# Threshold attention and a MetaFormer block on one core: layer-norm averages by token halves, and new places for the sums, squares and root around them

## The chip, the cores and the metric

One NeuronCore of a Trainium2 chip runs the whole program. The metric is the device time of one execution in microseconds; the table below gives the median of three. The core's engines run their own instruction streams in parallel: TensorE (PE in the profile; PEld is its loading of weights), VectorE (DVE), ScalarE (ACT), GpSimd (POOL) and SyncE (SP, which issues the transfers, DMAs). Work is handed from one engine to another by semaphores; SBUF is the on-chip memory, and PSUM the eight banks into which PE writes.

## The reference

Shapes: `q`, `k`, `v` are 8 batches x 8 heads x 576 tokens x 64; `x` is 8 x 576 x 512; `w_ch1` is 512 x 2048 and `w_ch2` 2048 x 512 (both weights arrive as 64-bit words and are converted in the kernel).

```python
scores = scale * np.matmul(q, k.transpose(0, 1, 3, 2))
thresh = np.max(scores, axis=-1, keepdims=True) - tau
scores = np.where(scores >= thresh, scores, -1000000000.0)
scores = scores - np.max(scores, axis=-1, keepdims=True)
attn = np.exp(scores)
attn = attn / (np.sum(attn, axis=-1, keepdims=True) + 1e-09)
attn_out = np.matmul(attn, v)
x = attn_out.transpose(0, 2, 1, 3).reshape(B, S, H * D)
mu = np.mean(x, axis=-1, keepdims=True)
var = np.mean((x - mu) ** 2, axis=-1, keepdims=True)
xn = (x - mu) / np.sqrt(var + 1e-06) * g_ln
ch = np.maximum(xn @ w_ch1, 0.0) @ w_ch2
return x + ch
```

## The kernel before

**Slots.** Attention runs in 72 slots, nine for each batch: four head pairs with the first 256 queries of each head, one slot with the last 64 queries of all heads, and four head pairs with the second 256. In a slot PE makes the scores (L434) into two PSUM tiles, `sc0` and `sc1`. DVE takes the row maximum, negated, of each (L450, `neg`). POOL makes thresholds from it (L454). ACT makes four exponentials (L463). DVE masks and sums them (L473, then two reciprocals), POOL divides (L490, four instructions), and DVE turns the result in 32 x 32 blocks (L559, two instructions). A DMA writes it to a scratch area in DRAM and another reads it back as `em`. In a later slot PE multiplies by the values (L638, L649), and at the begin of the slot after that ACT copies the two halves of the result to `x` (L663). One of these copies stands behind the first row maximum, at the place called "copy". POOL adds up the features (L692, `sums`), for the mean.

**Groups.** The MetaFormer block runs over 16 groups of `TOK` = 288 tokens, two for each batch, with features on the partitions (`NK` = 4 pieces of 128) and tokens along the rows. For a group `g`:

- `mean_of` (L701) multiplies the sums by `avg_sb`, a 128 x 128 matrix of 1/512, so that every partition gets the mean of each token. `product` (L98) does this in two matmuls, each for half of the output partitions, over all 288 tokens. The result stays in PSUM, and `centre` (L708) subtracts it from `x` with four DVE instructions.
- For groups 0 and 1, `first_part` (L988) makes the 16 pieces of `hidden` = relu(xc @ w_ch1) by plain products: `p1`, four products each, which ACT carries through a relu to `hidden` (L983, or L1008 for these two groups).
- From group 2 on, `first_units` (L955) makes eight pieces by plain `p1`s and eight by two units (`UNITS`), each in a slot of its own (`unit_slots`). A unit is a 2 x 2 product by Winograd's form of Strassen's scheme: seven products in place of eight, on sums and differences of the weights (`sums_of_w1` makes those once, during group 1) and of `xc` (`sum_x`, L859, makes `t1` to `t4`, two on DVE and two on POOL). Its results are brought together by DVE (L911) and ACT.
- The variance: ACT squares `xc` (L951), three POOL additions sum the four pieces (L953), PE averages them (L942), ACT adds epsilon and copies to SBUF (L944), and takes a logarithm and an exponential (L945, L946) for 1/sqrt. `root` (L776) refines that by one Newton step of three DVE instructions.
- `second_quarters` (L1046) makes hidden @ w_ch2 in seven `segment`s of 16 products of 144 tokens, again by Winograd's form. Sums of `hidden` (L1076) and of results (L1116) go to DVE and POOL, and `finish` (L1122) multiplies by `rb` and adds `x`; the results leave by `store`.

**The order.** The program fixes the order of instructions on each engine (`manual_schedule`, L149). The loop at L1326 goes through the slots, and `second_part` (L1222) deals steps of the group's generator `ffn_steps` into four quarters of each slot, after `STEPS` (the step count of each group), `ROOM` and `owed`. A generator yields a code and a cost after each step; unit steps stand in quarters 2 and 3 for the most part. `at_quarter(n, i, fn)` puts a call at a quarter of slot `n`; places -3, -2 and -1 stand around the scores, ahead of the row maximum. `later` (L1060) lines up DVE and POOL operations of the second part in `drops`; `drip` (L724) lets them go where there is room, and `need` (L1069) forces those that the next segment reads. `aside` holds calls that the loop lets go at fixed places (L1361, L1374, L1414, L1433), and `root` is one of them.

`ps_ff` has two PSUM buffers. Every `p1`, unit result, segment, mean and variance takes one of them in turn, so a product waits until the one before the last has been carried out. While `banks_taken` (L1134 to L1172) holds, means are put off to `waiting_mean`.

What `group_ready` (L1271) sets up for a group, in the slot ahead and in its first slot, is this:

```python
            at_quarter(*before, mean_of, g)
            at_quarter(*(first if g and first[1] else before), centre, g)
            if g > 1:
                at_quarter(first[0], 3 if first[1] else -1, sum_x, g)
        at_quarter(*first, lambda: queue.append(ffn_steps(g)))
```

From group 2 on, `ready` (L1215) is the begin of a slot, so `first` is that slot's quarter 0 and `before` the last quarter of the slot ahead; the two units stand in the slot `first[0]` and the one after it, called the first and the second unit slot below. So `mean_of` and `centre` run in the last quarter of the slot ahead, and `sum_x` at place -1 of the first unit slot, hence ahead of that slot's first row maximum on DVE. In group 1 the mean and `centre` are put among the steps of group 0 (`among`).

Of the kernel before, what the change touches and what calls it, by code (L numbers as in the profile page):

```python
# [18 lines left out]
def kernel(  # L19
# [679 lines left out]
    waiting_mean, banks_taken, among = [], [False], []  # L699

    def mean_of(g):  # L701
# [22 lines left out]
    def drip(room=None, everything=False):  # L724


        urgent = [i for i, d in enumerate(drops) if d[0]]
        n = urgent[-1] + 1 if urgent else 0
        room = dict(room or {})
        while drops:  # L730
            _, when, eng, cost, go = drops[0]
# [43 lines left out]

    def root(y, x, t):  # L776


        nc.vector.scalar_tensor_tensor(
            out=t, in0=y, scalar=-0.5, in1=y, op0=ALU.mult, op1=ALU.mult  # L780
        )
        nc.vector.tensor_mul(t, t, x)
        nc.vector.scalar_tensor_tensor(out=y, in0=t, scalar=1.5, in1=y, op0=ALU.add, op1=ALU.mult)
        rooted.append(y)

    rooted = []
    HT, HD, HM = TOK // 2, ND // 2, NK // 2
    early, late = slice(0, HT), slice(HT, TOK)
    w2 = {
# [68 lines left out]

    def sum_x(g):  # L859


        while g - 1 not in last_added:
            drops.pop(0)[-1]()
        xc = centred[g]
        part_of = lambda i, j: xc[:, 2 * i : 2 * i + 2, (early, late)[j]]
        (b11, b12), (b21, b22) = ([part_of(i, j) for j in range(2)] for i in range(2))
        t1, t2, t3, t4 = (
            ffn.tile([128, HM, HT], F32, tag="part", bufs=4, name=f"t{i}") for i in range(1, 5)
        )
        for eng, out, a, b in (  # L870
            (nc.vector, t1, b12, b11), (nc.gpsimd, t3, b22, b12),
            (nc.vector, t2, b22, t1), (nc.gpsimd, t4, b21, t2),
        ):
            eng.tensor_tensor(out=out, in0=a, in1=b, op=ALU.subtract)
        sums_of_x[g] = t1, t2, t3, t4

# [73 lines left out]
    def squares(sq, xc):  # L950
        nc.scalar.activation(sq, xc, func=AF.Square)  # L951
        for c in range(1, NK):
            nc.gpsimd.tensor_tensor(out=sq[:, 0], in0=sq[:, 0], in1=sq[:, c], op=ALU.add)  # L953

    def first_units(g):  # L955
# [32 lines left out]
    def first_part(g):  # L988


        xc = centred.pop(g)
        rb = sq = None
        plain = g == 0
        sums_of = differences() if g == 1 else iter(())
        for d in range(ND):
            while conversion.carried < 4 * (d // 4 + 1):
                yield 0, 0
            while d == ND - 2 and len(rooted) <= g and not plain:
                run_all(aside)
# [8 lines left out]
            nc.scalar.activation(hidden[:, d], p1, func=AF.Relu)  # L1008
            next(sums_of, None)
            yield 2, 1  # L1010
            if sq is None and d and (part > 1 or d == ND // 2 - 1):
                squared = d
                sq = hidden[:, ND - NK :]
                squares(sq, xc)
            elif sq is not None and rb is None and (
                d >= squared + (7 if plain else 3) and part > (0 if plain else 1)
                or d == ND - NK - 1
            ):
                two = [sq[:, c] for c in (2, 3)]
                if plain:  # L1020
                    two = [ffn.tile([128, HM, HT], F32, tag="part", bufs=4, name="two") for _ in two]
                    two = [t.rearrange("p m t -> p (m t)") for t in two]
                rb = variance(sq, two)
                yield 1, 1
        for _ in sums_of:
# [20 lines left out]
    def second_quarters(g, rb):  # L1046
# [13 lines left out]
        def later(*calls, urgent=None):  # L1060
            for what, cost, fn, eng, *args in calls:
# [4 lines left out]

                drops.append((urgent, now, eng, cost, go))

# [127 lines left out]
    ROOM = (0.6, 1.0, 1.25, 0.35)  # L1196
    STEPS = [1 + NK * ND * 2] + [1 + NK * ND * 2 - NK * ND // 8] + [
        1 + NK * ND * 2 - NK * ND // 8 - 2 * len(UNITS)
    ] * (NG - 2)
# [71 lines left out]
    def group_ready(g):  # L1271
# [203 lines left out]
```

## Time and profile before

| | us |
|---|---|
| median of three runs | 1356.83 |
| lowest and highest of them | 1356.06, 1356.85 |
| the profiled execution, its own time | 1358.76 |
| its span in the profile | 1357.0 |

| line, engine | what | count | busy, us | mean, ns |
|---|---|---|---|---|
| L434 PE | scores | 2048 | 139.7 | 403 |
| L638 PE | value products | 2368 | 130.9 | 265 |
| L103 PE | `seg` with `hidden` and w_ch2 | 3840 | 244.4 | 287 |
| L103 PE | `p1` and other first products of 288 | 2752 | 329.6 | 390 |
| L103 PE | `chain` of the units on `t` | 896 | 65.1 | 288 |
| L450 DVE | row maximum | 144 | 188.4 | 1349 |
| L473 DVE | mask and sum | 288 | 222.6 | 811 |
| L559 DVE | turning in blocks | 113 | 164.0 | 1452 |
| L463 ACT | exponentials | 288 | 195.6 | 752 |
| L490 POOL | division | 264 | 204.8 | 789 |
| L1128 POOL | `finish`, the product | 43 | 45.1 | 1048 |

How to read it: busy time is the sum over instructions of a line and a tile; the mean of one matmul holds its overlap with the next, since matmuls are pipelined. The profile also says for each instruction how long its engine stood idle ahead of it and which instruction of which engine released it. Times in a timeline count from the span's start. Two instructions on different engines that are shown at the same time did run side by side. The granted TensorE clock was 0.994 of full speed in the profiled execution.

### The profile page before, as it was taken

To read this page: it belongs to the slowest core of one execution; us is meant where nothing else is said; L and a number is where in the kernel's file an instruction comes from. 1 tells how busy PE (TensorE), PEld (TensorE's weight loads), DVE (VectorE), ACT (ScalarE), POOL (GpSimd) and SP (SyncE) were. 2 spreads that over 40 slices of the span, in tenths; PEclk is the share of its full clock that TensorE was granted. 3 is DMA by queue.
4 is the path that set the end of the run, shared out by engine and by line. 5 is a ranking of instruction groups with operands and counts; after the bars stand their busy time and mean duration, and the time that the engine had idled before them with its cause. 6 is when DMAs were issued, how large, how long until landed. Compare 5 with 4: busy or idle time off the path is not lost. (4 is left out here: it accounts for less than half of the span.)

```text
span 1357.0 us, 43410 instructions
## 1 busy us (share of the span) xinstructions
PE 1298.3 (96%) x18648; PEld 1052.8 (78%) x18648; DVE 959.7 (71%) x1700; ACT 479.3 (35%) x1051; POOL 651.6 (48%) x880
## 2 busy tenths in 40 slices
PE   8899899889999999999999999999999999999997
PEld 7765457769788797878879797887878788797977
DVE  7879885776867677776867768686777778677223
ACT  5866332142332414333332423324143333324120
POOL 3566555644545363454534455353634545444323
PEclk9999999999999999999999999999999999999999
DMA  8946864346744665545745467446664456453211
GB/s 159 299 114 170 214 175 151 140 135 191 193 150 146 185 166 167 188 150 128 204 150 185 138 190 192 150 146 186 166 179 170 149 134 187 150 185 115 80 19 19
DMA packets 335311, 214.11 MB, mean 158 GB/s; under 512 B 247376, under 2 KB 292688, under 8 KB 327056
## 3 DMA queue, kind: packets, MB, share of 16 engines
q1 hardware_dynamic: 329008, 210.46, 53.4%
q8 instruction: 146, 2.39, 0.7%
q10 hardware_dynamic: 5952, 0.74, 0.4%
q0 software_dynamic: 160, 0.15, 0.1%
q14 instruction: 45, 0.37, 0.1%
HBM read 124.00 MB, written 87.29 MB: 156 GB/s over the span
## 5 line engine op out<-in xcount | busy, mean ns | idle before, releaser
L103 PE MATMUL p<-xc,w 128*64 128x288 f32 (+1 forms) x2752 | 329.6, 390 | 17.0 <-ACT hidden L983 14.6
L103 PEld LDWEIGHTS p<-xc,w 128*64 128x64 f32 x2752 | 188.5, 137 | 143.6 <-ACT hidden L983 25.0
L450 DVE TENSOR_REDUCE neg<-sc 128x2 f32<-128x1152 f32 x144 | 188.4, 1349 | 108.7 <-PE sc L434 108.2
L490 POOL TENSOR_SCALAR e<-e,den 128x576 f32<-128x576 f32 x264 | 204.8, 789 | 119.3 <-DVE den L478 119.2
L103 PE MATMUL seg<-hidden,w 128*64 128x144 f32 x3840 | 244.4, 287 | 1.8 <-DVE hidden L1076 1.2
L103 PEld LDWEIGHTS seg<-hidden,w 128*64 128x64 f32 x3840 | 234.6, 137 | 11.6 <-issue 9.3
L473 DVE SCALAR_TENSOR_TENSOR e<-sc,thr,e 128x576 f32<-128x576 f32 x288 | 222.6, 811 | 22.4 <-POOL thr L454 10.5
L454 POOL TENSOR_SCALAR thr<-neg,low_sb 128x2 f32<-128x2 f32 x144 | 39.4, 274 | 347.7 <-DVE neg L450 347.5
L463 ACT ACTIVATE e<-sc,neg 128x576 f32<-128x576 f32 x288 | 195.6, 752 | 20.2 <-DMA scr<-e 13.3
L559 DVE STREAM_TRANSPOSE e<-e 128x1152 f32<-128x1152 f32 (+1 forms) x113 | 164.0, 1452 | 25.4 <-POOL e L490 24.6
L434 PE MATMUL sc<-kT,qT 64*64 64x384 f32 (+3 forms) x2048 | 139.7, 403 | 2.0 <-DVE e L473 1.6
L638 PE MATMUL sc<-em,v_in 128*64 128x128 f32 (+1 forms) x2368 | 130.9, 265 | 3.5 <-DMA em<-scr 2.9
L103 PE MATMUL seg<-hidden,stage 128*64 128x144 f32 x1920 | 126.0, 289 | 3.6 <-ACT part L1091 3.6
L638 PEld LDWEIGHTS sc<-em,v_in 128*64 128x64 f32 x2368 | 123.2, 138 | 6.3 <-issue 2.1
L103 PEld LDWEIGHTS seg<-hidden,stage 128*64 128x64 f32 x1920 | 119.0, 138 | 6.4 <-ACT part L1091 3.9
L1091 ACT COPY part<-seg 128x288 f32<-128x288 f32 x74 | 29.7, 405 | 229.0 <-PE seg L103 229.0
L434 PEld LDWEIGHTS sc<-kT,qT 64*64 64x64 f32 x2048 | 76.4, 133 | 43.0 <-issue 21.3
L663 ACT COPY x<-sc 128x128 f32<-128x128 f32 x120 | 31.6, 265 | 197.4 <-DVE neg L450 103.4
L1076 POOL TENSOR_TENSOR hidden<-hidden 128x576 f32<-128x576 f32 x60 | 84.0, 1419 | 24.6 <-ACT hidden L983 12.1
L1076 DVE TENSOR_TENSOR hidden<-hidden 128x576 f32<-128x576 f32 x60 | 52.5, 895 | 45.4 <-PE seg L103 39.0
L1128 POOL TENSOR_TENSOR y<-y,rb 128x288 f32<-128x288 f32 (+1 forms) x43 | 45.1, 1048 | 54.3 <-DVE y L1116 54.2
L103 PE MATMUL chain<-t,extra 128*64 128x144 f32 x896 | 65.1, 288 | 0.8
(163 smaller groups left out, 1615.9 us busy)
## 6 DMA issues: line engine op xcount, KB each, us to landing
scr<-e SPq DMA_DIRECT2D x60, 1152.0 KB, 5.0
em<-scr SPq DMA_DIRECT2D x63, 1024.0 KB, 5.7
out_dram<-ot SPq DMA_DIRECT2D x248, 36.0 KB, 3.9
q_in<-in_q_dram SPq DMA_DIRECT2D x120, 72.0 KB, 2.6
er<-scr SPq DMA_DIRECT2D x132, 64.0 KB, 5.2
k_in<-in_k_dram SPq DMA_DIRECT2D x116, 72.0 KB, 2.8
v_in<-in_v_dram SPq DMA_DIRECT2D x28, 256.0 KB, 5.5
w<-in_moe_w_ch_dram SPq DMA_DIRECT2D x10, 512.0 KB, 9.0
```

The lines of the kernel that those rows point to most:

```text
L103: nc.tensor.matmul(out[r], lhsT=lhsT[:, r], rhs=rhs, **flags)
L434: mm = nc.tensor.matmul(sc[h][64 * i : 64 * i + 64, at : at + n], lhsT=ql[r] if s == HP else qT[r, half, j * 128 + 64 * i : j * 128 + 64 * ...
L450: nc.vector.tensor_reduce(out=neg[:, i], in_=pairs[h], axis=AXL.X, op=ALU.max, negate=True,)
L454: nc.gpsimd.tensor_scalar(out=thr[:, i], in0=neg[:, i], scalar1=-1.0, scalar2=low_sb, op0=ALU.mult, op1=ALU.add,)
L463: nc.scalar.activation(blocks_of(es, i, n), like(blocks[i], n), func=AF.Exp, bias=neg[:, i : i + 1])
L473: nc.vector.scalar_tensor_tensor(out=e, in0=like(blocks[i], n), scalar=thr[:, i : i + 1], in1=e, op0=ALU.is_ge, op1=ALU.mult, accum_out=de ...
L490: nc.gpsimd.tensor_scalar(out=e, in0=e, scalar1=den[:, i : i + 1], scalar2=1.0, op0=ALU.mult, op1=ALU.mult,)
L559: nc.vector.transpose(et[:, :, at], et[:, :, at])
L638: mm = nc.tensor.matmul(dst[64 * h : 64 * h + 64], lhsT=vt[:, h, c, :], rhs=pick(em[:, 2 * j : 2 * j + 2, c], h), start=c == 0 and first, ...
L663: nc.scalar.copy(x_of(2 * b + (s > HP))[:, s % (HP + 1), 128 * j : 128 * j + 128], pv[j])
L1076: eng.tensor_tensor(out=out[at], in0=in0[at], in1=in1[at], op=op)
L1128: eng.tensor_tensor(out=z, in0=z, in1=r, op=ALU.mult)
```

## The change

It leaves what is computed as it is, and touches five things.

1. **Averages by token halves.** `average` replaces `product` for mean and variance. Each of its two matmuls takes 64 columns of `avg_sb` and 144 of the 288 tokens, so that the lower 64 partitions of the bank hold the early tokens' average and the upper 64 the late ones'. `spread` brings them to all 128 partitions of an SBUF tile, by four ACT instructions of 64 x 144; the variance's add epsilon at the same time, which took an instruction of its own. The mean is written over the sums that it came from (`spare` keeps the tile for the variance). In groups 0 and 1 the variance's average shares a bank with a `p1` (columns `TOK` and on), between its third and fourth product.
2. **`sum_x`** is called in two parts: `t1`, `t2`, `t3` on DVE, in the quarter of `centre` and behind it; `t4` on POOL in quarter 1 of the first slot. It waits there, by `drops`, for the last addition of the group before.
3. **Squares** go from the unit to the first unit slot's begin: ACT's square at place -3, two POOL sums at -1, the third in quarter 1. `root` works in place, in three DVE instructions as before, and is put at quarter 3 of the second unit slot (behind that slot's turning), in place of `aside`, which is emptied at the end of the first unit slot (L1433), ahead of the next row maximum on DVE.
4. **`sums_of_w1`** goes on by a piece in every 13th step of group 1's second part, not in every 8th.
5. **Around them:** `centre` lets go all of `drops` up to the additions "22" and "u4" of the group before; the last segment yields the bank for a waiting mean after 8 steps, not 12, and takes one more buffer in turn ("passed") behind the mean; the variance's step costs 0.5 and not 1, in `STEPS` too.

```diff
+    def average(to, bank, rhs, start, bias=None):
+        for h in range(2):
+            nc.tensor.matmul(
+                bank[64 * h : 64 * h + 64], lhsT=avg_sb[:, 64 * h : 64 * h + 64],
+                rhs=rhs[:, (early, late)[h]], start=start, stop=True, skip_group_check=True,
+            )
+        def spread():
+            for at in range(2):
+                for h in range(2):
+                    nc.scalar.activation(
+                        to[64 * at : 64 * at + 64, (early, late)[h]], bank[64 * h : 64 * h + 64],
+                        func=AF.Identity, **({"bias": bias[64 * h : 64 * h + 64]} if bias is not None else {}),
+                    )
+        return spread
+
     def mean_of(g):
...
-        means[g] = ps_ff.tile([128, TOK], F32, tag="ff", name="mean")
-        product(means[g], lhsT=avg_sb, rhs=sums.pop(g), start=True, stop=True)
+        bank = ps_ff.tile([128, HT], F32, tag="ff", name="mean")
+        means[g] = spare[g] = sums.pop(g)
+        average(means[g], bank, means[g], True)()
...
     def centre(g):
...
         mean = means.pop(g)
+        while any(d[4] in ("22", "u4") for d in drops):
+            drops.pop(0)[-1]()
...
-    def root(y, x, t):
+    def root(y, x):
+        nc.vector.tensor_mul(x, x, y)
         nc.vector.scalar_tensor_tensor(
-            out=t, in0=y, scalar=-0.5, in1=y, op0=ALU.mult, op1=ALU.mult
+            out=x, in0=x, scalar=-0.5, in1=y, op0=ALU.mult, op1=ALU.mult
         )
-        nc.vector.tensor_mul(t, t, x)
-        nc.vector.scalar_tensor_tensor(out=y, in0=t, scalar=1.5, in1=y, op0=ALU.add, op1=ALU.mult)
-        rooted.append(y)
+        nc.vector.scalar_tensor_tensor(out=y, in0=x, scalar=1.5, in1=y, op0=ALU.add, op1=ALU.mult)
...
-    def sum_x(g):
-        while g - 1 not in last_added:
-            drops.pop(0)[-1]()
+    def sum_x(g, which):
...
-        for eng, out, a, b in (
-            (nc.vector, t1, b12, b11), (nc.gpsimd, t3, b22, b12),
-            (nc.vector, t2, b22, t1), (nc.gpsimd, t4, b21, t2),
-        ):
-            eng.tensor_tensor(out=out, in0=a, in1=b, op=ALU.subtract)
-        sums_of_x[g] = t1, t2, t3, t4
+        t = sums_of_x.setdefault(g, [])
+        for i in which:
+            if i == 3:
+                while g - 1 not in last_added:
+                    drops.pop(0)[-1]()
+            t.append(ffn.tile([128, HM, HT], F32, tag="part", bufs=4, name=f"t{i + 1}"))
+            eng, a, b = (
+                (nc.vector, b12, b11), (nc.vector, b22, t[0]), (nc.vector, b22, b12),
+                (nc.gpsimd, b21, t[min(i, 1)]),
+            )[i]
+            eng.tensor_tensor(out=t[i], in0=a, in1=b, op=ALU.subtract)
...
-    def variance(sq, two):
-        var = ps_ff.tile([128, TOK], F32, tag="ff", name="var")
-        product(var, lhsT=avg_sb, rhs=sq[:, 0], start=True, stop=True)
+    def variance(g, sq):
+        x = spare.pop(g)
+        bank = ps_ff.tile([128, HT], F32, tag="ff", name="var")
+        average(x, bank, sq[:, 0], True, eps_sb)()
         rb = ffn.tile([128, TOK], F32, tag="rb", bufs=2, name="rb")
-        nc.scalar.activation(two[0], var, func=AF.Identity, bias=eps_sb)
-        nc.scalar.activation(rb, two[0], func=AF.Ln)
+        nc.scalar.activation(rb, x, func=AF.Ln)
         nc.scalar.activation(rb, rb, func=AF.Exp, scale=-0.5)
-        aside.append(lambda: root(rb, *two))
+        at_quarter(now // QUARTERS + 1, 3, root, rb, x)
         return rb
...
-                if g not in sums_of_x:
-                    sum_x(g)
-                if k == 0:
-                    squares(sq, xc)
                 yield from unit(g, xc, k)
                 k += 1
                 if k == 1:
-                    rb = variance(sq, [sq[:, c] for c in (2, 3)])
-                    yield 2, 1
+                    rb = variance(g, sq)
+                    yield 2, 0.5
...
-            p1 = ps_ff.tile([128, TOK], F32, tag="ff", name="p1")
+            bank = ps_ff.tile([128, 512], F32, tag="ff", name="p1")
+            p1 = bank[:, :TOK]
             for c in range(NK):
+                if due and c == NK - 1:
+                    x = spare.pop(g)
+                    spread = average(x, bank[:, TOK : TOK + HT], sq[:, 0], False, eps_sb)
+                    yield 1, 0.5
...
-        for _ in range(12):
+        for _ in range(8):
             yield next(last)
         banks_taken[0] = False
         while waiting_mean:
             mean_of(waiting_mean.pop(0))
+            ps_ff.tile([128, HT], F32, tag="ff", name="passed")
...
-            if i % 8 == 7:
+            if i % 13 == 12:
                 next(sums, None)
...
             if g > 1:
-                at_quarter(first[0], 3 if first[1] else -1, sum_x, g)
+                sq = hidden[:, ND - NK :]
+                at_quarter(*before, sum_x, g, (0, 1, 2))
+                at_quarter(
+                    first[0], -3,
+                    lambda: nc.scalar.activation(sq, centred[g], func=AF.Square),
+                )
+                at_quarter(first[0], -1, add_squares, sq, 1, 2)
+                at_quarter(first[0], 1, add_squares, sq, 3)
+                at_quarter(first[0], 1, sum_x, g, (3,))
```

More of the change, by code (lines that the diff above doesn't have):

```diff
@@ L699 @@
     waiting_mean, banks_taken, among = [], [False], []
+    HT = TOK // 2
+    early, late = slice(0, HT), slice(HT, TOK)
+    def average(to, bank, rhs, start, bias=None):
[12 more added lines that the diff above has]
+        return spread
     def mean_of(g):
@@ L704, in mean_of @@
             return
-        means[g] = ps_ff.tile([128, TOK], F32, tag="ff", name="mean")
-        product(means[g], lhsT=avg_sb, rhs=sums.pop(g), start=True, stop=True)
+        bank = ps_ff.tile([128, HT], F32, tag="ff", name="mean")
+        means[g] = spare[g] = sums.pop(g)
+        average(means[g], bank, means[g], True)()
+    spare = {}
     def centre(g):
@@ L730, in drip @@
         while drops:
-            _, when, eng, cost, go = drops[0]
+            _, when, eng, cost, _, go = drops[0]
             if n <= 0 and not everything:
@@ L774, in send @@
             )
-    def root(y, x, t):
+    def root(y, x):
+        nc.vector.tensor_mul(x, x, y)
         nc.vector.scalar_tensor_tensor(
-            out=t, in0=y, scalar=-0.5, in1=y, op0=ALU.mult, op1=ALU.mult
+            out=x, in0=x, scalar=-0.5, in1=y, op0=ALU.mult, op1=ALU.mult
         )
-        nc.vector.tensor_mul(t, t, x)
-        nc.vector.scalar_tensor_tensor(out=y, in0=t, scalar=1.5, in1=y, op0=ALU.add, op1=ALU.mult)
-        rooted.append(y)
-    rooted = []
-    HT, HD, HM = TOK // 2, ND // 2, NK // 2
-    early, late = slice(0, HT), slice(HT, TOK)
+        nc.vector.scalar_tensor_tensor(out=y, in0=x, scalar=1.5, in1=y, op0=ALU.add, op1=ALU.mult)
+    HD, HM = ND // 2, NK // 2
     w2 = {
@@ L866, in sum_x @@
         (b11, b12), (b21, b22) = ([part_of(i, j) for j in range(2)] for i in range(2))
-        t1, t2, t3, t4 = (
-            ffn.tile([128, HM, HT], F32, tag="part", bufs=4, name=f"t{i}") for i in range(1, 5)
-        )
-        for eng, out, a, b in (
-            (nc.vector, t1, b12, b11), (nc.gpsimd, t3, b22, b12),
-            (nc.vector, t2, b22, t1), (nc.gpsimd, t4, b21, t2),
-        ):
-            eng.tensor_tensor(out=out, in0=a, in1=b, op=ALU.subtract)
-        sums_of_x[g] = t1, t2, t3, t4
+        t = sums_of_x.setdefault(g, [])
[9 more added lines that the diff above has]
+            eng.tensor_tensor(out=t[i], in0=a, in1=b, op=ALU.subtract)
     def unit(g, xc, k):
@@ L938, in unit, with add_squares @@
         yield 2 if k else 3, 0.5
-    def variance(sq, two):
-        var = ps_ff.tile([128, TOK], F32, tag="ff", name="var")
-        product(var, lhsT=avg_sb, rhs=sq[:, 0], start=True, stop=True)
+    def variance(g, sq):
+        x = spare.pop(g)
+        bank = ps_ff.tile([128, HT], F32, tag="ff", name="var")
+        average(x, bank, sq[:, 0], True, eps_sb)()
         rb = ffn.tile([128, TOK], F32, tag="rb", bufs=2, name="rb")
-        nc.scalar.activation(two[0], var, func=AF.Identity, bias=eps_sb)
-        nc.scalar.activation(rb, two[0], func=AF.Ln)
+        nc.scalar.activation(rb, x, func=AF.Ln)
         nc.scalar.activation(rb, rb, func=AF.Exp, scale=-0.5)
-        aside.append(lambda: root(rb, *two))
+        at_quarter(now // QUARTERS + 1, 3, root, rb, x)
         return rb
-    def squares(sq, xc):
-        nc.scalar.activation(sq, xc, func=AF.Square)
-        for c in range(1, NK):
+    def add_squares(sq, *which):
+        for c in which:
             nc.gpsimd.tensor_tensor(out=sq[:, 0], in0=sq[:, 0], in1=sq[:, c], op=ALU.add)
@@ L992, in first_part @@
         rb = sq = None
+        due = False
         plain = g == 0
@@ L997, in first_part @@
                 yield 0, 0
-            while d == ND - 2 and len(rooted) <= g and not plain:
-                run_all(aside)
-            p1 = ps_ff.tile([128, TOK], F32, tag="ff", name="p1")
+            bank = ps_ff.tile([128, 512], F32, tag="ff", name="p1")
+            p1 = bank[:, :TOK]
             for c in range(NK):
+                if due and c == NK - 1:
+                    x = spare.pop(g)
+                    spread = average(x, bank[:, TOK : TOK + HT], sq[:, 0], False, eps_sb)
+                    yield 1, 0.5
                 product(
@@ L1008, in first_part @@
             nc.scalar.activation(hidden[:, d], p1, func=AF.Relu)
+            if due:
+                due = False
+                spread()
+                rb = ffn.tile([128, TOK], F32, tag="rb", bufs=2, name="rb")
+                nc.scalar.activation(rb, x, func=AF.Ln)
+                nc.scalar.activation(rb, rb, func=AF.Exp, scale=-0.5)
+                aside.append(lambda: root(rb, x))
             next(sums_of, None)
@@ L1013, in first_part @@
                 sq = hidden[:, ND - NK :]
-                squares(sq, xc)
+                nc.scalar.activation(sq, xc, func=AF.Square)
+                add_squares(sq, 1, 2, 3)
             elif sq is not None and rb is None and (
@@ L1018, in first_part @@
             ):
[L1019 to L1024, printed above, removed]
+                due = True
         for _ in sums_of:
@@ L1065, in go @@
                     done.add(what)
-                drops.append((urgent, now, eng, cost, go))
+                drops.append((urgent, now, eng, cost, what, go))
         def need(*what):
@@ L1196 @@
     ROOM = (0.6, 1.0, 1.25, 0.35)
-    STEPS = [1 + NK * ND * 2] + [1 + NK * ND * 2 - NK * ND // 8] + [
-        1 + NK * ND * 2 - NK * ND // 8 - 2 * len(UNITS)
+    STEPS = [0.5 + NK * ND * 2] + [0.5 + NK * ND * 2 - NK * ND // 8] + [
+        0.5 + NK * ND * 2 - NK * ND // 8 - 2 * len(UNITS)
     ] * (NG - 2)
```

## The prediction

> **What bounds the kernel now.** First the page's table of busy time: TensorE (PE) is the only engine near its limit.
>
> ```profile
> PE 1298.3 (96%) x18648; PEld 1052.8 (78%) x18648; DVE 959.7 (71%) x1700; ACT 479.3 (35%) x1051; POOL 651.6 (48%) x880
> ```
>
> So only two things are worth time: PE work taken away, and PE's idle time (58.7 us). Second, the view of waits for PE, its two largest rows (in all, times, longest):
>
> ```profile
> PE p L103 <- ACT hidden L983: 14.6, 26, 3.0
> PE chain L103 <- ACT hidden L983: 6.8, 12, 0.6
> ```
>
> PE wants a bank of `ps_ff` (two buffers) whose last product ScalarE (ACT) hasn't yet carried through L983. Third, the timeline of a group of odd number, on each engine, shows why ACT is late (start, busy, instruction, idle before and releaser):
>
> ```profile
> 663.76 2.12 PE L434 MATMUL sc<-kT,qT 64*64 64x384 f32 x32
> 665.81 4.10 PE L103 MATMUL p<-xc,w 128*64 128x288 f32 x32
> 670.50 1.20 PE L103 MATMUL chain<-xc,w 128*64 128x144 f32 x16 [0.59 <-ACT hidden L983]
> 672.07 1.20 PE L103 MATMUL p<-xc,w 128*64 128x144 f32 x16 [0.36 <-ACT hidden L983]
> 673.41 1.20 PE L103 MATMUL chain<-t,extra 128*64 128x144 f32 x16
> ...
> 680.96 2.12 PE L434 MATMUL sc<-kT,qT 64*64 64x384 f32 x32
> ```
>
> ```profile
> 664.68 1.66 DVE L874 TENSOR_TENSOR t<-xc 128x288 f32<-128x288 f32 x1
> 666.37 0.94 DVE L874 TENSOR_TENSOR t<-xc,t 128x288 f32<-128x288 f32 x1
> 667.23 2.61 DVE L450 TENSOR_REDUCE neg<-sc 128x2 f32<-128x1152 f32 x2
> ...
> 683.99 0.46 DVE L783 SCALAR_TENSOR_TENSOR rb<-hidden,rb 128x288 f32<-128x288 f32 x1
> 684.37 2.61 DVE L450 TENSOR_REDUCE neg<-sc 128x2 f32<-128x1152 f32 x2
> ...
> 701.35 2.62 DVE L450 TENSOR_REDUCE neg<-sc 128x2 f32<-128x1152 f32 x2 [5.53 <-PE sc L434]
> ```
>
> In the slot at 699.19 VectorE (DVE) is free: the row maximum begins 2.16 us after the scores begin, the first exponential 3.71 after, and PE never waits. In a group's first unit slot it begins 3.47 after (667.23), behind `sum_x` (L874); in the second 3.41 after (684.37), behind the root (L779 to L783). These 1.3 us pass on through the exponentials, which stand ahead of L983 on ACT.
>
> The price by start times, three `p1` at 701.24 to 707.11 giving 1.957 us each and 16 records of the unit 0.98. Odd groups: 0.78 + 0.59 + 0.36 + 0.05 = 1.78 us in the first unit slot (665.81 + 3.91 against 670.50, and so on), 0.72 + 0.58 + 0.06 = 1.36 in the second. Even groups: 0.90 (589.61 to 603.25) and 0.76 (609.86 to 617.47), since four and three `p1` stand ahead of their units. Below, an even slot is one of groups 2 to 14 (seven), an odd one of groups 3 to 13 (six); group 15 runs in the tail.
>
> **The averages.** PE spends 0.48 us on a mean (583.98 to 584.46), as much on a variance; two matmuls of 144 columns cost what one product of `seg` does, 16 records in 0.98, so 0.24. That two halves with different right sides run side by side is seen at L638: 32 records of 128 columns take 1.75, the same rate. Saved: 0.24 each. Four ACT spreads are new: no row shows 64x144, the rows below and above are 128x64 (0.215) and 128x288 (0.405); I take 0.27, near 128x128 (0.265), so 1.1 us a time, between 0.9 and 1.6.
>
> For the mean this lies in ACT's idle time: in the old trace ACT waits 5.83 us ahead of 663.69. The four subtractions of centring now start after the spread. In the slot ahead of an even group (16.5 us, scores at 571.09): mean done 12.85 after its scores, spread 13.95, four subtractions of 0.42, three sums of 0.45 (L874's 0.42 and 0.46 in the tail), done at 17.05. The next scores begin at 16.22 and the maximum at 18.4: 1.3 us to spare. Ahead of an odd group it is 1.8. That cover pays for the third sum (from POOL to DVE) too; without it each lost 0.1 us puts back 0.1 us of stall a group.
>
> A rule speaks against this: the Trainium skill, "GPSIMD Engine Reference", section "1. Specifications", says that POOL shares its SBUF interfaces with VectorE and contends with DVE instructions that have two SBUF inputs, which centring now becomes. The trace has that: 1.66 us at 664.68, beside a POOL add, against 0.42 at 1294.88 without one. By the rule with POOL busy throughout, centring would take 4 x 1.66 = 6.6 us, past all cover, and the sum below would lose its stalls; but POOL idles there (nothing from 658.7 to 662.9), and the two large POOL operations that followed (L1128, L1116 on 128x576) now stand behind the squares.
>
> **Even groups.** The first two sums of squares stand ahead of the thresholds on POOL: the square starts after the copy of `p3` (0.33 after the scores), ends at 1.5, two adds of 0.81 end at 3.2, the first threshold comes at 3.5: hidden. The maximum begins on time, so 0.90 and 0.76 vanish. The variance's longer tail on ACT ends 2.6 after the next scores, ahead of the exponential at 3.71. Root moved behind the turning falls into DVE's idle stretch (5.53 ahead of 701.35 in its like); nothing needs `rb` before the second half.
>
> **Odd groups, where I expect a new wait.** The changed order puts on POOL, between the second threshold and the divisions L490: scaling q 0.74, the last square 0.85, the two on 128x576 1.6 and 1.5, the fourth sum 0.85. These rows stand in the old trace at other places:
>
> ```profile
> 662.88 1.56 POOL L1128 TENSOR_TENSOR y<-y,rb 128x576 f32<-128x576 f32 x1 [4.19 <-DVE y L1116]
> 664.51 1.50 POOL L1116 TENSOR_TENSOR y<-y,x 128x576 f32<-128x576 f32 x1
> ...
> 673.62 1.46 POOL L490 TENSOR_SCALAR e<-e,den 128x576 f32<-128x576 f32 x2 [2.69 <-DVE den L478]
> ...
> 678.63 1.38 DVE L911 TENSOR_TENSOR hidden<-sc,hidden 128x288 f32<-128x288 f32 x3
> ```
>
> Counted from the scores: the second threshold starts at 4.88 (2.72 after the maximum, as at 669.95) and ends at 5.13; POOL is free at 10.7, DVE's two reciprocals at 9.0 and 10.7 (L1116 for `p3` moved ahead of them, 0.6). The four divisions run 10.7 to 13.6, the two transposes (1.38) end at 15.0, and the unit's sums L911 (1.93 for all four) end at 16.9; old: 16.25. PE without its stalls would be through the unit at 14.6. It now waits for the first L911 (15.5, the bank of the variance), then, as the changed order pulls one `p1` forward, for ACT L934, which needs L911: 16.95. Next scores: 16.95 + 1.96 + 0.27 = 19.2, less the pulled `p1` 17.2: the old 17.20. Gain nothing, where 1.78 + 0.24 were to be had. Bounds: 2.0 if POOL is not in the way, minus 0.6 if each POOL step takes the longest row seen of its kind (1.0 for the 0.85s, 1.6 for both large ones).
>
> In the second odd slot one `p1` is left ahead of the unit. Its `p2` waits for L983 until 3.71 + 1.73 = 5.44 (as 668.77 to 670.50), wanted at 4.99: 0.45; the chain waits for L905 until 7.0, wanted at 6.42: 0.59. With 1.04 in place of 1.36 the gain is 0.32, between 0 and 1.36.
>
> **The rest.** Wider w_ch1's sums move DVE and POOL work of equal size; stalls of 3.6, 1.2, 2.4 and 3.0 us lie there (238 to 276). They are DVE's chain; what shortens it for certain is its end: adds, centring and sums took 7.46 us (265.37 to 272.83) beside POOL and would take 5.0. I take 2.4, between 0 and 10.3. In groups 0 and 1 the averages inside a `p1` save two 0.24s and perhaps 1.3 of stalls, but PE then waits longer for the weights (4.08 at 153): 0, between -1 and +2. In the tail PE's 0.57 wait for `part` ahead of 1291.90 goes, as the next product takes the mean's bank: 0.6.
>
> **Sum.** Even first slots 6 x 0.90 = 5.4 (group 2's is in the 2.4); even second 7 x 0.76 = 5.3; variances of even groups 7 x 0.24 = 1.7; means of groups 3 to 15, 13 x 0.24 = 3.1; odd second 6 x 0.32 = 1.9; odd first 0; group 1's end 2.4; tail 0.6. Together 20.4 us. The profiled execution took 1358.76 (span 1357.0 and 1.8 around it), 1.9 above the median of 1356.83; the gain is taken from the median: **1336.4**.
>
> **Rivals.** (a) POOL isn't in the way in odd groups, as it runs these steps beside DVE's: 6 x 2.0 = 12 more, 1324. For it: the divisions waited 2.69 for DVE before; against: the four steps sum to 4.8. (b) The maximum stays late, because four ACT instructions and centring from SBUF use up the 1.3 us: half of the stalls (6.3) stay, 1343. For it: ACT's spread has no row of its own; against: ACT and POOL idle there. (c) The wait merely changes its place, in even groups too: all but the PE work returns, 1352 to 1357. (d) Slower: POOL's steps ahead of the divisions are stretched by DVE. At 85.28 four divisions took 4.59 beside DVE where 2.91 is usual, 1.6 times; 4.8 us would become 7.7, 2.9 later. Odd slots lose 6 x 2.9, even ones, whose transposes have 1.45 of cover ahead of L911, 7 x 1.45: 27.5 against 20.4, so 1364; it decides from 2.4 us of stretch on. Against it: beside L473 at 578.6 the divisions kept 2.90.
>
> **How the numbers follow.** My forecast 0.58 (own range 1330 to 1341), (a) 0.16, (b) 0.13, (c) 0.04, (d) 0.09. The range runs from (a) to just past (b), 1323 to 1346, with (c) and (d) left out. About 0.2% (2.7 us) is what a measurement of this kernel tells from no change: faster 0.88, within 0.03, slower 0.09.
>
> **What would show it.** Right: L450 begins 2.2 us after L434 in every unit slot; PE's waits for L983 shrink from 21.4 us to about 6; mean and variance take 0.24; in odd first slots PE waits for L911 and L934 and the divisions start 10.7 after the scores. Wrong: L490 before 10 there (then (a)), L450 later than 2.5 ((b)), L911 past 18 ((d)).

## The result, and the profile after

The changed kernel takes 1337.57 us (median of four runs, 1336.1 to 1338.82) against 1356.84 before: 0.9857 of it, 95% interval 0.984 to 0.9874, so 19.3 us less. The forecast was 1336.4. Its profiled execution took 1336.10 (span 1334.0), the fastest of the four, and the one before 1358.76 (span 1357.0), slower than all four of its kernel, so the traces show 23.0 us of difference where the medians show 19.3.

The page's table of busy time: PE keeps the same number of instructions and loses 13.1 us of busy time, and POOL 10.7; ACT has 112 instructions more.

```profile
PE 1285.2 (96%) x18648; PEld 1052.7 (79%) x18648; DVE 947.3 (71%) x1714; ACT 515.0 (39%) x1163; POOL 640.9 (48%) x866
```

The view of waits for PE (in all, times, longest). The relu of `p1` is now L1002, the relu at a unit's end L958, the first chain copy L929:

```profile
...
PE p L103 <- ACT hidden L958: 4.8, 7, 0.7
PE sc L103 <- DVE e L473: 4.3, 6, 0.9
...
PE p L103 <- ACT hidden L1002: 2.9, 7, 1.4
...
PE chain L103 <- ACT hidden L929: 2.1, 6, 0.3
```

The 14.6 and 6.8 us of waits for the relu of `p1` are down to 2.9. Two new waits stand in their place, six and seven times: a unit's product waits for VectorE's masks (L473), and the `p1` that was pulled forward waits for the unit's last relu. Six of each belong to the odd groups' first unit slots (the seventh of the second stands in the tail), as PE's timeline of the same group as before shows (start, busy, instruction, idle before and releaser):

```profile
652.08 2.12 PE L434 MATMUL sc<-kT,qT 64*64 64x384 f32 x32
...
660.11 1.15 PE L103 MATMUL chain<-t,extra 128*64 128x144 f32 x16
661.94 1.20 PE L103 MATMUL sc<-t,w 128*64 128x144 f32 x16 [0.68 <-DVE e L473]
...
667.66 0.41 PE L708 MATMUL var<-hidden,avg_sb 128*64 128x144 f32 x4
668.78 2.16 PE L103 MATMUL p<-xc,w 128*64 128x288 f32 x16 [0.71 <-ACT hidden L958]
...
671.14 2.12 PE L434 MATMUL sc<-kT,qT 64*64 64x384 f32 x32
```

By start times the first wait is 661.94 - 660.11 - 0.98 = 0.85 and the second 668.78 - 667.66 - 0.24 = 0.88. DVE and POOL in the same slot tell where the masks were held up:

```profile
654.23 2.62 DVE L450 TENSOR_REDUCE neg<-sc 128x2 f32<-128x1152 f32 x2 [1.71 <-PE sc L434]
...
658.81 1.60 DVE L1142 TENSOR_TENSOR y<-y,part 128x288 f32<-128x288 f32 x1
660.33 0.81 DVE L473 SCALAR_TENSOR_TENSOR e<-sc,thr,e 128x576 f32<-128x576 f32 x1
```

```profile
657.21 0.74 POOL L350 TENSOR_SCALAR q_in<-q_in,scl_sb 128x576 f32<-128x576 f32 x1
657.92 0.80 POOL L976 TENSOR_TENSOR hidden<-hidden 128x288 f32<-128x288 f32 x1
658.67 1.42 POOL L1154 TENSOR_TENSOR y<-y,rb 128x576 f32<-128x576 f32 x1
660.17 1.51 POOL L1142 TENSOR_TENSOR y<-y,x 128x576 f32<-128x576 f32 x1
661.64 0.79 POOL L899 TENSOR_TENSOR t<-xc,t 128x288 f32<-128x288 f32 x1
662.42 2.90 POOL L490 TENSOR_SCALAR e<-e,den 128x576 f32<-128x576 f32 x4
```

The row maximum begins at 2.15 after the scores. The addition of the last segment (L1142 on DVE, 658.81) takes 1.60 us, four times its usual 0.42, and ends just after POOL's product (658.67 to 660.09). The divisions begin at 662.42, 10.34 after the scores.

Where the time came from, slot by slot (start of the scores to start of the next; slots counted from 0, as in the experiments below). The four rows from the even first unit slot to the other five slots stand for six such stretches each; with them the table makes up 22.6 of the 23.0 us:

| place | before | after | difference | foreseen |
|---|---|---|---|---|
| slots 0 to 13 | 226.62 to the end of slot 13 | 227.09 | +0.5 | 0 |
| slots 14 to 16 (group 1's end, group 2's first unit) | 64.85 | 59.27 | -5.6 | -2.4, and -0.2 for the variance |
| even first unit slot (34) | 20.25 | 19.08 | -1.17 | -0.90 - 0.24 |
| even second (35) | 19.59 | 18.84 | -0.75 | -0.76 |
| odd first and second (38, 39) | 35.43 | 35.05 | -0.38 | -0.32 |
| the other five slots of nine (two means) | 82.88 | 82.41 | -0.47 | -0.48 |
| from slot 71 to the end | 115.80 | 114.89 | -0.9 | -1.6 |

The first row gives the time at which slot 14 begins. It is the least steady part: among this study's profiles of kernels that are nearly alike up to there, it lay between 225.94 and 228.95, while most of the later slots repeat to some hundredths (a few single ones take up to some 1.2 us longer in one trace or another).

### The profile page after: what moved, and what is told of

Same layout as the page of the kernel before. It is cut to its first block, busy times and chain, and to the rows that moved or that the text cites. A ratio compares the mean times of both kernels' runs of the same rounds, so it can differ in the third digit from the quotient of the medians.

```text
span 1334.0 us, 43429 instructions
## 1 busy us (share of the span) xinstructions
PE 1285.2 (96%) x18648; PEld 1052.7 (79%) x18648; DVE 947.3 (71%) x1714; ACT 515.0 (39%) x1163; POOL 640.9 (48%) x866
## 4 chain that ended last, share of the span: by engine, by line
PE 72%; DVE 8%; POOL 7%; SPq 4%; ACT 4%; issue 3%; DMA 2%; POOLq 0%; DVEq 0%; ACTq 0%
PE seg L103 29%; PE p L103 15%; PE sc L434 9%; PE sc L638 7%; PE chain L103 6%; PE sc L103 3%; POOL e L490 2%; DVE neg L450 2%; ACT e L463 2%; PE sc L649 2%; SPq L120 1%; DVE e L473 1%; DVE extra L569 1%; DVE hidden L935 1%; DVE e L559 1%
## 5 line engine op out<-in xcount | busy, mean ns | idle before, releaser
L473 DVE SCALAR_TENSOR_TENSOR e<-sc,thr,e 128x576 f32<-128x576 f32 x288 | 222.5, 810 | 12.7 <-POOL thr L454 5.2
L454 POOL TENSOR_SCALAR thr<-neg,low_sb 128x2 f32<-128x2 f32 x144 | 46.3, 322 | 359.2 <-DVE neg L450 358.8
L976 POOL TENSOR_TENSOR hidden<-hidden 128x288 f32<-128x288 f32 x48 | 38.7, 807 | 77.9 <-ACT hidden L1311 76.4
L1002 ACT ACTIVATE hidden<-p 128x288 f32<-128x288 f32 x112 | 47.2, 422 | 50.9 <-PE p L103 50.7
```

The lines of the kernel that those rows point to most:

```text
L454: nc.gpsimd.tensor_scalar(out=thr[:, i], in0=neg[:, i], scalar1=-1.0, scalar2=low_sb, op0=ALU.mult, op1=ALU.add,)
L473: nc.vector.scalar_tensor_tensor(out=e, in0=like(blocks[i], n), scalar=thr[:, i : i + 1], in1=e, op0=ALU.is_ge, op1=ALU.mult, accum_out=de ...
```

## The experiments

Every kernel is the changed one with one edit (the third and the ninth are combinations) and was timed against the kernel before. The changed kernel's ratio is 0.9857.

**1. POOL's two large steps behind the divisions.** In the first unit slot, the search for the group before's last addition leaves POOL's product and addition on 128x576 ("hi") in the list.

```diff
                 while g - 1 not in last_added:
-                    drops.pop(0)[-1]()
+                    drops.pop(drops[0][4] == "hi")[-1]()
```

> The two large POOL steps of the group before (the product with rb and the addition of x, both 128x576) go behind the divisions in each first unit slot; nothing else moves. Theory: in the odd groups' first unit slots POOL's order sets the end. The addition on DVE no longer runs beside POOL's product, so the masks begin 7.2 us after the scores in place of 8.25, the divisions at 8.9 in place of 10.34, and the unit's sums end 1.5 earlier. Of PE's two waits there, that for the scores' tile (0.85 by start times) goes and that for the unit's last relu (0.88) falls to about 0.2; the slot takes 17.6 in place of 19.06, and 6 such slots give 9 us: 1328.5. Even groups' first slots (19.08, no wait) stay. Rival: the wait is set by ACT's chain and the order on PE, whatever POOL does first: slot 18.9 or more, time 1336 to 1339.

Measured: 1330.4, ratio 0.9801 (0.9787 to 0.9814). Slot 38 takes 17.86. DVE's timeline there, with the scores at 649.00:

```profile
655.73 0.41 DVE L1142 TENSOR_TENSOR y<-y,part 128x288 f32<-128x288 f32 x1
656.07 0.81 DVE L473 SCALAR_TENSOR_TENSOR e<-sc,thr,e 128x576 f32<-128x576 f32 x1
```

With no product on POOL at that moment the same addition takes 0.41; the masks begin at 7.07 and the divisions at 8.93, as expected. The wait for the masks is gone from PE; that for the last relu is 0.58 by start times, where 0.2 was expected, so the slot stays 0.26 above the 17.6 that was worked out and the time 2 us above. Even first slots stay at 19.08, though their divisions too come 2.6 earlier: there they have cover. So POOL's order set the end of the odd first slot in the changed kernel, and the rival falls.

**2. The pulled `p1` put back.** The variance's step counts 1 for groups 2 to 15.

```diff
-                    yield 2, 0.5
+                    yield 2, 1
...
-        0.5 + NK * ND * 2 - NK * ND // 8 - 2 * len(UNITS)
+        1 + NK * ND * 2 - NK * ND // 8 - 2 * len(UNITS)
```

> The variance's step counts 1 again and not 0.5 for groups 2 to 15, so in the odd groups one p1 goes back from the first unit slot to the second; averages, sums, squares and root stay as changed. Theory: the p1 pulled forward pays twice, by waiting for the unit's last relu in the first slot (0.88) and by leaving a single p1 ahead of the second unit (0.99 of waits there). With it back the first slot takes 16.4 to 16.7 (its scores wait some 0.4 for the unit's sums that read their tile) and the second 16.95 without a wait: 33.5 for the two in place of 35.05, 6 times, 1328.5. Rival: the wait only moves to the next scores and comes back whole: 34.9 to 35.1 for the two, 1336 to 1339.

Measured: 1327.85, ratio 0.9782 (0.9769 to 0.9795). Slots 38 and 39 take 16.59 and 17.04, 33.6 for the two. Half a step in a table of costs had moved one `p1` by a slot, at a price of 1.4 us in each odd group.

**3. Both edits together.**

> Both edits, POOL's two large steps behind the divisions and the p1 back in the second slot. Theory: the waits of both odd unit slots go, 15.4 and 16.95, 32.35 in place of 35.05; 6 x 2.7 = 16 us: 1321. Rival (the two gains are one and the same wait): as the better of the two alone, 1328 to 1330; or, if neither matters, 1336 to 1339.

Measured: 1321.29, ratio 0.973 (0.9716 to 0.9743). The odd pair takes 15.38 and 17.04 (slots 20 and 21) with no wait. The gains add up, 7.2 and 9.7 alone, 16.3 together. In one group slot 39 takes 18.03: ACT's first exponential waits 0.94 there for the `scr` transfer that still reads the attention weights' tile, so there a transfer is next. This is the fastest version of the study, with experiment 9, from which it can't be told apart.

**4. Squares back in the unit.** The square and three POOL sums run behind the exponentials and divisions again.

```diff
+                if k == 0:
+                    nc.scalar.activation(sq, xc, func=AF.Square)
+                    add_squares(sq, 1, 2, 3)
                 yield from unit(g, xc, k)
...
-                at_quarter(
-                    first[0], -3,
-                    lambda: nc.scalar.activation(sq, centred[g], func=AF.Square),
-                )
-                at_quarter(first[0], -1, add_squares, sq, 1, 2)
-                at_quarter(first[0], 1, add_squares, sq, 3)
```

> The squares and their three POOL sums go back to where they stood, into the unit's slot behind the exponentials and the divisions. Theory (the squares' move is worth little by itself, since POOL's time ahead of the divisions is what counts): in odd first slots the divisions begin 0.8 earlier, 9.5, and the wait for the last relu shrinks by 0.8, while ACT's square of 1.2 ahead of the chain's copy adds 0.4 to 0.5 of wait there: about -2 us in all, even slots plus or minus 0.2: 1333 to 1339. Rival (the move is what made the even slots free of waits): ACT's square delays the chain's copy in all 13 first slots by 1.2 or the variance comes late: 1345 to 1353.

Measured: 1332.47, ratio 0.9816 (0.9802 to 0.9829), a little better than the theory's range. The divisions of slot 38 begin at 9.60 and the slot takes 18.33; even first slots take 19.19, 0.11 more. So this part of the change, by itself, makes the changed kernel slower: it puts POOL work ahead of divisions that set the end.

**5. The root back ahead of the row maximum.**

```diff
-        at_quarter(now // QUARTERS + 1, 3, root, rb, x)
+        aside.append(lambda: root(rb, x))
```

> The root goes back to the end of the first unit slot, ahead of the next row maximum on DVE; all else as changed. Theory: DVE's order decides. In even groups rb now comes 3.29 us after the second unit slot's scores (the variance has four spreads on ACT where it had one copy), so the root ends at 4.7 and the maximum, which began at 2.16, begins at 4.7; that is 1.3 later than in the kernel before, where the wait was 0.76, so some 2.0 a group, 7 times 2.0 = 14. In odd groups rb comes 0.87 after the scores and the root is done by 2.3: nothing. Time 1347 to 1353. Rival: three p1 stand ahead of the unit and hide it, as does ACT's own lateness: 1336 to 1341.

Measured: 1352.77, ratio 0.9965 (0.9953 to 0.9976). DVE and PE in slot 35, scores at 603.34:

```profile
606.66 0.46 DVE L806 TENSOR_TENSOR sum<-sum,rb 128x288 f32<-128x288 f32 x1 [3.54 <-ACT rb L970]
...
608.03 2.62 DVE L450 TENSOR_REDUCE neg<-sc 128x2 f32<-128x1152 f32 x2
```

```profile
611.30 2.16 PE L103 MATMUL p<-xc,w 128*64 128x288 f32 x16 [1.81 <-ACT hidden L1002]
```

DVE idles 3.54 us for `rb`, the maximum begins 4.69 after the scores, and PE loses 2.0: the slot takes 20.87 for 18.84. Odd second slots lose 0.1. 15 us hang on this one place. That is more than the root cost in the kernel before (0.76 a group), since `rb` now comes later, behind the four spreads.

**6. Averages over 288 tokens again.** The mean is read from PSUM, the variance brought over by one ACT instruction.

```diff
-        bank = ps_ff.tile([128, HT], F32, tag="ff", name="mean")
-        means[g] = spare[g] = sums.pop(g)
-        average(means[g], bank, means[g], True)()
+        means[g] = ps_ff.tile([128, TOK], F32, tag="ff", name="mean")
+        spare[g] = sums.pop(g)
+        product(means[g], lhsT=avg_sb, rhs=spare[g], start=True, stop=True)
...
-        bank = ps_ff.tile([128, HT], F32, tag="ff", name="var")
-        average(x, bank, sq[:, 0], True, eps_sb)()
+        var = ps_ff.tile([128, TOK], F32, tag="ff", name="var")
+        product(var, lhsT=avg_sb, rhs=sq[:, 0], start=True, stop=True)
+        nc.scalar.activation(x, var, func=AF.Identity, bias=eps_sb)
```

> From group 2 on (and all means) an average is one product of 288 tokens again, the mean read by centring from PSUM, the variance brought over by one ACT instruction; groups 0 and 1 keep the variance inside a p1. All else as changed. Theory: PE's work alone counts, 0.24 each: 14 means and 7 variances of even groups cost 5.0 more, variances of odd groups nothing, as PE waits behind them for the unit's last relu anyway: 1341 to 1344. Rival: the four spreads on ACT, and centring from SBUF beside POOL, eat up what PE saves: 1335 to 1338.5.

Measured: 1340.95, ratio 0.9876 (0.9856 to 0.9896), whose interval overlaps that of the changed kernel. The slots decide: 0.24 more in each slot with a mean (37: 19.89 for 19.65) and in each even first slot (19.32 for 19.08), nothing in the odd first (19.05), where PE waits behind the variance anyway. The four spreads cost nothing where they stand.

**7. w_ch1's sums in every 8th step again.**

```diff
-            if i % 13 == 12:
+            if i % 8 == 7:
```

> w_ch1's sums go on in every 8th step of group 1's second part again; all else as changed. Theory: the spread is what took the waits for DVE and the sums of hidden out of group 1's second part (6.0 of waits in slots 14 and 15 before, 3.3 after): 3 to 5 us come back, 1340 to 1343. Rival: the gain there came from the averages, centring and sums of x at its end, and the spread itself only moves equal work: 1335 to 1339.

Measured: 1338.96, ratio 0.9859 (0.9839 to 0.9878). Slots 14 to 16 take 24.03, 15.63 and 19.65, together 59.31, against 20.91, 15.25 and 23.12, 59.28. The spread moves a wait from slot 14 to slot 16 and gains nothing, as the rival had it.

**8. Sums of x behind the last addition.** `t1` to `t3` are put at the first unit slot's begin, behind the addition of the last segment, as they stood before; all three stay on DVE.

```diff
-            if i == 3:
-                while g - 1 not in last_added:
-                    drops.pop(0)[-1]()
+            while g - 1 not in last_added:
+                drops.pop(drops[0][4] == "hi")[-1]()
+            while i == 3 and any(d[4] == "hi" for d in drops):
+                drops.pop(0)[-1]()
...
-                at_quarter(*before, sum_x, g, (0, 1, 2))
+                at_quarter(first[0], -1, sum_x, g, (0, 1, 2))
```

> t1 to t3 go behind the addition of the group before's last segment on DVE (as they stood in the kernel before), at the first unit slot's begin, all three still on DVE and POOL's order as changed. This sets the place apart from the neighbour: before, the three DVE steps (0.64, 1.66, 0.94) ran beside POOL. Theory of contention: with POOL idle until 1.4 us after the scores the addition and the sums take 0.42 + 3 x 0.45 from 0.65 on, the maximum begins at 2.2 to 2.6, and hardly a wait comes back; in odd slots the addition no longer stands ahead of the masks beside POOL's product, so the wait for the scores' tile (0.85) shrinks: 1331 to 1338. Theory of place, which the prediction used: being behind the last segment's copy is what makes the maximum late: it begins at 3.4, 0.9 comes back in 7 even and about 0.5 in 6 odd slots: 1344 to 1348.

Measured: 1340.15, ratio 0.987 (0.9848 to 0.9893), between the two theories; the interval overlaps that of the changed kernel, so the slots decide. DVE and POOL in slot 34, scores at 578.67 (this kernel's lines are one higher):

```profile
579.03 0.46 DVE L1143 TENSOR_TENSOR y<-y,part 128x288 f32<-128x288 f32 x1 [0.68 <-ACT part L1118]
579.40 0.45 DVE L900 TENSOR_TENSOR t<-xc 128x288 f32<-128x288 f32 x1
579.89 0.46 DVE L900 TENSOR_TENSOR t<-xc,t 128x288 f32<-128x288 f32 x1
580.26 1.05 DVE L900 TENSOR_TENSOR t<-xc 128x288 f32<-128x288 f32 x1
581.24 2.61 DVE L450 TENSOR_REDUCE neg<-sc 128x2 f32<-128x1152 f32 x2
```

```profile
580.13 1.84 POOL L977 TENSOR_TENSOR hidden<-hidden 128x288 f32<-128x288 f32 x2 [5.59 <-ACT hidden L1312]
```

The maximum begins 2.57 after the scores. The steps take 0.45 until POOL starts, and then one takes 1.05. Even first slots lose nothing (19.08). Odd ones lose 0.34 (19.40). There the masks begin earlier, 7.14, and PE's wait for them is gone; but the maximum and with it POOL's thresholds come 0.42 later, the two large steps still stand behind these, and the divisions begin at 10.66 in place of 10.34. So the divisions set the end of the odd first slot, and the wait for the masks doesn't. And in the kernel before it was not the place of the sums alone that made the maximum late, but that they ran beside POOL: the first two sums took 1.66 and 0.94 there and take 0.45 and 0.46 here.

**9. Experiment 3 with w_ch1's sums in every 11th step.**

```diff
-            if i % 13 == 12:
+            if i % 11 == 10:
```

> On top of both edits (POOL's large steps behind the divisions, the p1 back): w_ch1's sums go on in every 11th step, not every 13th, so that no piece of them stands between the masks and the turning of the slot ahead of group 2. Theory: there DVE waited for POOL (3.2 us in two waits) to make such a piece, which made the turning, centring and the first p1 of group 2 late (2.47 and 1.38 of waits on PE); slot 16 falls from 23.2 to about 20.5, and the time to 1318. Rival: as with every 8th step, the same waits come back in slot 14 (20.9 to 24): 1320 to 1323.

Measured: 1320.43, ratio 0.9727 (0.9711 to 0.9743), no different from experiment 3. Slot 16 falls to 21.04, as the theory has it, but slots 14 and 15 grow to 21.45 and 16.78: 59.27 for the three, the same sum with a third spread. The rival holds.

**10. POOL's two large steps beside centring.** `centre` lets go of "hi" too.

```diff
-        while any(d[4] in ("22", "u4") for d in drops):
+        while any(d[4] in ("22", "u4", "hi") for d in drops):
```

> POOL's two large steps of the group before go to the quarter of centring, where POOL idles 6.4 us, and so run beside DVE's centring and sums; all else as changed. Theory of contention: DVE steps with two SBUF inputs take about 1.0 and not 0.42 beside POOL, so centring and sums end some 3 us later and use up the 1.3 to 1.7 of cover: the maximum begins 3.0 to 4.0 after the scores in both kinds of first slot; even slots lose 0.9, while odd ones gain 1.2 as their divisions begin at 8.9: 1333 to 1340. Rival (no contention): the maximum stays at 2.16 and the time is that of POOL's steps behind the divisions, 1329 to 1332.

Measured: 1334.37, ratio 0.983 (0.9814 to 0.9846). DVE and POOL ahead of slot 38 (scores at 653.67):

```profile
651.33 3.15 DVE L742 TENSOR_TENSOR xc<-x,sum 128x288 f32<-128x288 f32 x4 [0.77 <-ACT sum L716]
```

```profile
650.26 1.57 POOL L1154 TENSOR_TENSOR y<-y,rb 128x576 f32<-128x576 f32 x1 [1.52 <-DVE y L1142]
651.91 1.51 POOL L1142 TENSOR_TENSOR y<-y,x 128x576 f32<-128x576 f32 x1
```

Centring takes 3.15 where it takes 1.56 with POOL idle. The contention is there, but not its price: 3.0 to 4.0 was expected for the maximum, and it is still on time in odd slots and begins at 2.74 in even ones, which costs these 0.09. The expectation had stretched every step; only two of the four are (0.82 and 1.67), and the other two take 0.44. Odd slots gain as in experiment 1 (17.87). Slot 16 lost 2.4, which is most of what the whole is behind experiment 1: there PE has no cover and waits for centring itself, 3.57 and 0.87 us in place of 2.37, as centring takes 3.97. So the contention did cost time, but in a place that the expectation didn't name; that the time lies in its range is luck.

**11. The bank's order.** The last segment gives way to a waiting mean after 12 steps again, and the extra turn of the bank ("passed") is left out.

```diff
-        for _ in range(8):
+        for _ in range(12):
...
-            ps_ff.tile([128, HT], F32, tag="ff", name="passed")
```

> The last segment makes 12 of its steps before it gives way to a waiting mean, as before, and the extra turn of the bank behind the mean is left out; all else as changed. Theory: the mean comes 0.1 (even groups) to 0.4 us (odd) later, which the cover of 1.3 and more hides, and the first p1 seldom waits for the segment's copy: 1336 to 1339. Rival: without the extra turn the first p1 of each group takes the bank that the segment's copy still holds, 0.3 to 0.6 in 14 groups: 1342 to 1346.

Measured: 1338.33, ratio 0.986 (0.9843 to 0.9876): no difference that shows, and the unit slots from 17 on agree to 0.04.

## Why the prediction was right

**The price of a late maximum.** Right to a few hundredths: -1.17 and -0.75 in even slots against -1.14 and -0.76. The sums of `xc` end 0.82 us after the next scores (578.86 against 578.04), as counted, and the maximum has 1.3 us to spare. That the root's place sets the even second slots is shown by experiment 5. For the even first slots the text named one cause too few. It had the maximum wait behind the sums; experiment 8 puts them back there, and the slots keep their 19.08. So what brought the 0.93 is not their place; what is left is that POOL's two large steps no longer run beside them, which no run undoes by itself. Nor does each 0.1 us beyond the cover cost 0.1 at once: a maximum at 2.57 costs nothing (experiment 8), one at 2.74 costs 0.09 (experiment 10), and the old 3.47 went with 0.93.

**The averages.** 0.24 each, shown by experiment 6; the new spreads took 0.29 each for the mean (1.17 for four), between the bounds, and 0.37 for the variance (1.53 for four). The variance's tail on ACT ends 3.29 after the next scores (600.41 against 597.12), not 2.6; the exponential still begins at 3.71.

**The new wait in odd first slots.** Right in size: next scores at 19.06 against a forecast 19.2, divisions at 10.34 against 10.7, PE's wait for the last relu as foreseen. One link was different. The text had PE wait for the unit's sums and then for the relu; PE was first held 0.85 earlier by the masks, because the last addition took 1.60 beside POOL's product and 0.6 had been put down for it. So one source, the two large POOL steps, delayed both DVE and the divisions; experiment 8, where the first delay is gone and the slot is no shorter, shows that only the second counts. Experiments 1 and 4 show that POOL's order is the cause, and experiment 2 that the `p1` pulled forward is the other half.

**Odd second slots.** PE waits 0.42 and 0.57 by start times for the relu of `p1` and the chain's copy; 0.45 and 0.59 were worked out. Over the whole span PE's waits for the relu of `p1` fell to 2.9, below the 6 that the text gave as a sign.

**Group 1's end** is the term that was mis-sized most: 2.4, and 0.2 for the variance, with a bound of 10.3, against 5.6 measured. The text counted only the end of DVE's chain. Experiments 7 and 9 show that the wider spread isn't where the rest came from: three spreads give 59.3 for the three slots. Undoing the averages gives back 2.8 there (slots 14 to 16 at 62.03), so part of it is theirs. With the squares back (experiment 4) the three slots take 59.39, with the sums of x late (8) 59.63, with the bank's old order (11) 59.33: little of it is theirs. Beside POOL's large steps (10) they take 61.69, so the time of centring and the sums counts here. Which of the edits that no run undoes (among them the third sum on DVE and the additions that `centre` lets go) brought the rest of some 2 us stays open. **The tail** gave 0.15 besides the second unit of group 14, not 0.6 and the mean's 0.24: PE waits 0.46 for L958 and 0.27 for centring in their place. **The total** is closer than its parts: by the traces the kernel gained 23.0 us, by the medians 19.3, and the forecast of 20.4 lies between them. That 1336.4 is within 1.2 us of the measured median is in part luck; the rows of the table are the better check.

**The rule on shared interfaces.** The Trainium skill, "GPSIMD Engine Reference", section "1. Specifications", spoke against centring from SBUF, and the prediction set it aside because POOL idles there. Both hold: with POOL idle centring took 1.56, and in experiment 10, beside POOL, 3.14 to 3.49 in groups 3 to 14 (not the 6.6 that the text priced, since only two of the four steps were held). It should have been applied to the last addition too, where a DVE step with two SBUF inputs now meets POOL. "Trainium Architecture — The Big Picture", section "What this means for kernel authors", calls the shared port an exclusive lock. The traces agree in shape: the addition at 658.81 ends 0.32 us after POOL's product, and in experiment 10 the first step of centring ends 0.32 after POOL's product (652.15 against 651.83), the second 0.32 after POOL's addition (653.74 against 653.42), and the last two run at their usual 0.44.

**Rivals.** (a), POOL not in the way, is what experiment 1 makes true by another order, for 7.2 us and not 12, since the pulled `p1` still pays; with experiment 2's edit it is 16. (b) and (c) did not come. (d) did not either: POOL's four steps ahead of the divisions took 4.5 us (657.92 to 662.42), not more than the 4.8 put down, and the divisions 2.90.

## What to carry to other kernels

Where one engine is busy 96% of the time, price each wait by start times in one stage of each kind, and follow every moved instruction on the engine that it is moved to: this change won some 5.3 us (7 times 0.75) in the even second slots by moving the root out of the row maximum's way and gave several back by moving other steps into the way of the divisions. In this case, dealing the same work out more widely (every 8th, 11th or 13th step) gained nothing. And cost a VectorE step with two SBUF inputs by what GpSimd does at that moment, not by its usual duration.

## What the runs showed of the hardware

A DVE step of 128x288 with two SBUF inputs that started beside one of POOL's two-input operations ended 0.31 to 0.32 us after that operation in each of these cases: 0.42 to 0.45 became 1.60 (slot 38), 1.66 (in the kernel before) and 1.05 (experiment 8). In experiment 10 one step was held for each POOL operation, so the four of centring went from 1.56 to 3.15 beside two of them. POOL lost less: its product on 128x576 took 1.42 in slot 38, where it began first, 1.41 in experiment 1, where it runs beside DVE's turning, and 1.57 in experiment 10, where a DVE addition was still running at its start. DVE's masks, which read one input from PSUM, kept 0.81 beside the same POOL steps.
